# Attention and two feed-forward layers on one core: the second layer's row products held back, token parts spread over two pairs, later narrowing of weights

## The chip, the core and the metric

The kernel runs on one core of a Trainium2 chip. The engines are TensorE (matmuls, PE, and its weight loads, PEld), VectorE (DVE), ScalarE (ACT), GpSimd (POOL) and SyncE (SP), which issues most DMAs. The metric is the device time of one execution in microseconds (us). Everything is computed in float32; the weights of the two feed-forward layers arrive as float64.

## The reference

```
x = landmark_attention(q, k, v)          # 4 batches, 8 heads, 576 tokens, 64 per head -> 2304 x 512
x = (sigmoid(x @ w_gate) * (x @ w_val)) @ w_out          # 512 -> 1536 -> 512
h = x @ w_in                                             # 512 -> 2048
out = (max(h, 0) + alpha * min(h, 0)) @ w_out2           # 2048 -> 512
```

The attention has 32 landmarks per head, three softmaxes and six Newton steps for a pseudo-inverse. The output is 2304 x 512.

## The kernel before

**Split operands.** A float32 operand of a large matmul is held as a high part (the value rounded to the fast matmul format, a copy on ScalarE, line 124) and a low part (value minus high part, line 125, on VectorE, or on GpSimd where `lo="pool"`). Each product is then three matmuls: low times high, high times low, high times high (`TERMS`).

**First stage (to about 496 us).** Attention of batch 0, then 96 steps. A step is one block of 128 hidden features for half a batch (288 tokens): 12 matmuls of the gate and value products (`gv`, line 647), sigmoid and product, split, and, two steps later, 12 matmuls of the first layer's output (`acc`, line 666). Beside the steps run the attentions of the later batches, folding of attention matrices into weights (`psf`), and the preparation of the second stage. Its output goes to DRAM (`x2d`).

**Narrowing.** The second feed-forward layer's weights are 32 blocks of float64. `narrow_w2` loads one (`raw2`, two buffers), turns it into float32 with one or two ScalarE and two or three VectorE instructions (lines 139 to 151, the last writes `n2`, one buffer), and stores it to DRAM (`w2d`). In the program's text they begin at step `NARROW_FROM` with one every `NARROW_EVERY` steps. The two buffers lie in `apool` up to step 54; at step 55 that pool is given back and they lie in `rpool`. `rpool` is given back at step 83, and the pool `q2pool` (four homes for token parts, `xo2`) takes its room.

**Second stage.** Three groups `i` of 768 tokens, eight pairs `g` each; a pair is two blocks of 128 hidden features. The first product `x @ w_in` of a pair, a 2 x 2 block product (two feature blocks, two token halves of 384, two halves of the contraction), is made with seven block products instead of eight (`ORDER7` = 1, 2, 6, 7, 5, 4, 3). Each (`product`, line 950) is six matmuls of 384 columns into one of two PSUM banks (`gv`); VectorE adds (`plus`, line 1008) and one ScalarE copy (line 1015) read it out and free the bank. Four results h11, h22, h21, h12 come out per pair; `activated` takes each through two ScalarE instructions (lines 962, 963), one VectorE instruction (964) and a split into `g2s` or `g2r`. Each result then gives three parts of the second layer (`behind2`), a part being three matmuls of 512 columns (line 991) into one of six banks that accumulate over all 16 feature blocks; `catch_up2(n)` emits up to n parts. After a group's last pair the six banks are copied out (`store`, line 933).

**Token parts.** A group's tokens are loaded as four blocks (`load_x`, at pair 6 of the group before, line 770). Four VectorE subtractions of 128 x 768 (line 783) make the sums that seven products need, and seven operands of two halves each are split: 14 parts (`make_x7`, lines 124 and 125), which rotate through 15 homes. For groups 1 and 2 all this is written after pair 7, and the low half of every second part is on GpSimd. Parts, weights and tokens are named `x`, `w` and `xf` in the trace.

**Order.** Each engine works off its instructions in one fixed order. That order isn't the text's: the framework lays the work out ahead of time by text position and by when it takes operands and buffers to be ready. So an instruction can stand far from its place in the text.

Of the kernel before, what the change touches and what calls it, by code (L numbers as in the profile page):

```python
# [21 lines left out]
def tile_landmark_attention_glu_prelu(  # L22
# [46 lines left out]
    X2_LOAD, X2_SPLIT = 6, 7  # L69

    NARROW_FROM, NARROW_EVERY = 36, 1.4
# [611 lines left out]
    ORDER7 = (1, 2, 6, 7, 5, 4, 3)  # L683
    PLACE7 = {1: (0, 0), 2: (0, 1), 6: (1, 0), 5: (1, 1), 7: (2, 0), 3: (2, 1), 4: (3, 0)}
# [66 lines left out]
    def load_x(i):  # L751

        def room(first):
            if i == 0:
                if first:
                    t = home([P, 2, HG], F32, "xf")
                    return t
                return ws_tile("xf", (P, 2, HG), F32)
            if first:
                return wpool.tile([P, 2, HG], F32, tag="raw", name="xf", bufs=4)  # L760
            return ws_tile("xf", (P, 2, HG), F32)

        bs = {}
        for j, th in ((0, 0), (0, 1), (1, 1), (1, 0)):
            t = room(j == 0)
# [10 lines left out]
        bs["T2"] = room(False)  # L776
        xf[i] = bs

    def make_x7(i, ops):
        b11, b12, b21, b22, t2 = (xf[i][n] for n in ((0, 0), (0, 1), (1, 0), (1, 1), "T2"))  # L780

        def sub(out, x, y):
            nc.vector.tensor_tensor(out=out, in0=x, in1=y, op=ALU.subtract)

        for op in ops:
            if op == 6:

                sub(b11, b12, b11)
                sub(t2, b22, b11)
                sub(b12, b22, b12)  # L790
            if op == 4:

                sub(b21, b21, t2)
            src = {1: b11, 2: b21, 6: t2, 5: b11, 7: b12, 4: b21, 3: b22}[op]
            for kk in range(2):
                t = home([P, 2, HG], F32R, "x7")
                x7[i, op, kk] = t
                split(t, src[:, kk], lo="pool" if i > 0 and kk else "dve")
# [61 lines left out]
    for b in range(B):  # L860
# [5 lines left out]
        for i, (half, f, f0, f1) in enumerate(order):  # L866
# [45 lines left out]
            if at == X2_AT[0]:  # L912
                load_x(0)
                make_x7(0, ORDER7[:4])
            if at == X2_AT[1]:
# [5 lines left out]
                make_x7(0, ORDER7[4:])  # L921
# [20 lines left out]
    def product(i, g, op):  # L942
# [5 lines left out]
        for a, e in TERMS:  # L948
            for kk in range(2):
# [4 lines left out]
                n += 1  # L954
        return ps[:, :HG]
# [3 lines left out]
    def activated(h, f):  # L959
# [8 lines left out]
        if turn2[0] % 3:  # L968
# [6 lines left out]
    accs2, count, behind2 = {}, {}, deque()  # L975

# [3 lines left out]
    def catch_up2(n):  # L980

        for _ in range(min(n, len(behind2))):
# [56 lines left out]
    for i in range(NG):  # L1039
        for g in range(NF2 // 2):  # L1040
# [7 lines left out]
            if i + 1 < NG and g == X2_LOAD:  # L1048
                load_x(i + 1)
            pair(i, g)  # L1050
            if i + 1 < NG and g == X2_SPLIT:
# [33 lines left out]
```

## Time and profile before

| | us |
|---|---|
| median of three runs | 913.55 |
| lowest, highest | 912.08, 916.63 |
| the profiled execution | 911.39 |
| its span, first to last instruction | 909.6 |
| of it: up to the first matmul of line 950 | 495.9 |
| of it: second stage's matmuls | 407.7 |

The page of the profile gives busy time by engine, the table of stretches gives the same for any piece of the span (start and end, length, then busy time and number of instructions of PE, PEld, DVE, ACT and POOL, the granted TensorE clock as a share of full speed, the DMA engines' busy share, GB/s), the list of waits says which engine stood idle until what, and the timeline shows instructions in order. A busy TensorE isn't a TensorE at its peak, since matmuls are pipelined and their ends are modelled. So the spacing of matmul starts in a long run is read beside it.

### The profile page before, as it was taken

The numbers are of one execution on the slowest core, as the hardware profiler recorded it, in microseconds if no ns is written. First come the engines' busy times: TensorE is split into PE (matmuls) and PEld (weight loads), VectorE is DVE, ScalarE is ACT, GpSimd is POOL, SyncE is SP. The second block draws the span as 40 slices with busy tenths as digits, with TensorE's granted clock in tenths as the row PEclk, the third lists the DMA queues.
The fourth block names the chain that finished last, engine by engine and source line by source line (L and its number), as shares of the span: only waits on it lengthen the run. The fifth ranks groups of instructions, "written<-read, shape, count | busy, mean of one in ns | idle before, by whom it ended". The sixth has DMA issues, their size and how long they took to land.

```text
span 909.6 us, 15881 instructions
## 1 busy us (share of the span) xinstructions
PE 852.3 (94%) x6017; PEld 711.6 (78%) x6017; DVE 585.6 (64%) x1214; ACT 456.4 (50%) x981; POOL 83.7 (9%) x84
## 2 busy tenths in 40 slices
PE   5689889899999999998999999998999998999996
PEld 4367667677887877898999888886888877888884
DVE  3789988587665343779755787757554557554544
ACT  6676864465554333656544555644443435443433
POOL 0221112111011000230000000002000003000000
PEclk9679989999999999999999999999999999999999
DMA  9676878978431242888446446436432435552002
GB/s 270 218 234 185 252 248 240 285 222 255 132 95 54 94 143 90 264 253 256 161 166 236 150 172 210 144 111 204 128 132 93 127 106 197 173 173 93 1 1 69
DMA packets 98603, 150.98 MB, mean 166 GB/s; under 512 B 37328, under 2 KB 58336, under 8 KB 98528
## 3 DMA queue, kind: packets, MB, share of 16 engines
q1 hardware_dynamic: 95072, 137.40, 47.4%
q0 software_dynamic: 3456, 12.58, 4.4%
q8 instruction: 47, 0.77, 0.3%
q14 instruction: 28, 0.23, 0.1%
HBM read 108.01 MB, written 41.94 MB: 165 GB/s over the span
## 4 chain that ended last, share of the span: by engine, by line
PE 76%; DVE 9%; ACT 5%; DMA 5%; issue 3%; POOL 1%; SPq 1%; DVEq 0%; ACTq 0%; POOLq 0%
PE o L991 20%; PE acc L666 15%; PE gv L647 15%; PE prod L950 15%; PE psf L609 3%; PE psq L200 2%; DMA raw<-in_moe_w_in_dram 2%; DVE h L964 1%; PE psc L219 1%; PE psz L412 1%; PE psa L219 1%; DVE raw L148 1%; DVE h L1008 1%; PE psv L323 1%; DMA tk<-in_k_dram 1%
## 5 line engine op out<-in xcount | busy, mean ns | idle before, releaser
L950 PE MATMUL prod<-x,w 128*128 128x384 f32 x1008 | 195.9, 340 | 7.7 <-DVE u L1008 6.7
L647 PE MATMUL gv<-A,we 128*128 128x288 f32 x1152 | 194.9, 309 | 5.9 <-ACT g L658 3.4
L950 PEld LDWEIGHTS prod<-x,w 128*128 128x128 f32 x1008 | 176.8, 188 | 22.0 <-DVE u L1008 16.2
L647 PEld LDWEIGHTS gv<-A,we 128*128 128x128 f32 x1152 | 164.2, 193 | 36.3 <-issue 24.5
L666 PE MATMUL acc<-gs,wconv 128*128 128x288 f32 x1152 | 183.1, 302 | 6.6 <-DVE gs L125 3.1
L666 PEld LDWEIGHTS acc<-gs,wconv 128*128 128x128 f32 x1152 | 162.5, 191 | 19.1 <-issue 6.8
L991 PE MATMUL o<-w,g2s 128*128 128x512 f32 x576 | 148.3, 401 | 2.0 <-ACT g2s L124 1.2
L991 PEld LDWEIGHTS o<-w,g2s 128*128 128x128 f32 x576 | 105.2, 189 | 33.2 <-ACT g2s L124 7.2
L962 ACT ACTIVATE n<-h 128x384 f32<-128x384 f32 x96 | 50.4, 525 | 138.5 <-DVE h L1008 138.5
L991 PE MATMUL o<-w,g2r 128*128 128x512 f32 x288 | 74.6, 398 | 2.5 <-ACT g2r L124 1.9
L964 DVE SCALAR_TENSOR_TENSOR h<-n,minus_alpha,h 128x384 f32<-128x384 f32 x96 | 61.7, 643 | 16.2 <-ACT h L963 12.8
L658 ACT ACTIVATE g<-gv 128x288 f32<-128x288 f32 x96 | 39.3, 409 | 60.3 <-PE gv L647 57.2
L659 DVE TENSOR_TENSOR g<-g,gv 128x288 f32<-128x288 f32 x96 | 43.2, 450 | 38.6 <-PE gv L647 37.4
L124 ACT CAST gs<-g 128x288 fp32r<-128x288 f32 x96 | 41.5, 432 | 49.5 <-DVE g L659 48.8
L991 PEld LDWEIGHTS o<-w,g2r 128*128 128x128 f32 x288 | 52.2, 188 | 18.1 <-ACT g2r L124 5.3
L125 DVE TENSOR_TENSOR gs<-g,gs 128x288 fp32r<-128x288 f32 x96 | 50.2, 523 | 21.6 <-ACT gs L124 21.4
L1008 DVE TENSOR_TENSOR h<-u,prod 128x384 f32<-128x384 f32 x72 | 39.8, 552 | 34.9 <-PE prod L950 32.3
L139 ACT ACTIVATE raw<-raw 128x512 f32<-128x512 f32 x68 | 46.2, 680 | 30.6 <-DMA raw<-in_moe_w_in_dram 16.9
L1008 DVE TENSOR_TENSOR h<-p,prod 128x384 f32<-128x384 f32 x24 | 13.3, 554 | 66.4 <-PE prod L950 64.6
L148 DVE SCALAR_TENSOR_TENSOR raw<-raw 128x512 uint32<-128x512 uint32 x68 | 49.2, 734 | 9.1 <-ACT raw L143 8.3
L963 ACT ACTIVATE h<-h 128x384 f32<-128x384 f32 x96 | 50.4, 525 | 2.6
L125 POOL TENSOR_TENSOR x<-xf,x 128x384 fp32r<-128x384 f32 x14 | 15.9, 1141 | 335.7 <-ACT x L124 218.3
(137 smaller groups left out, 926.8 us busy)
## 6 DMA issues: line engine op xcount, KB each, us to landing
w<-w7d SPq DMA_DIRECT2D x48, 512.0 KB, 4.1
raw<-in_moe_w_out_dram SPq DMA_DIRECT2D x28, 512.0 KB, 4.9
wgv<-wgvd POOLq DMA_DIRECT2D x24, 512.0 KB, 5.0
w7d<-w SPq DMA_DIRECT2D x24, 512.0 KB, 2.7
raw<-in_moe_w_in_dram SPq DMA_DIRECT2D x16, 512.0 KB, 4.7
w2d<-n SPq DMA_DIRECT2D x32, 256.0 KB, 2.7
raw<-in_moe_w_gate_dram SPq DMA_DIRECT2D x24, 256.0 KB, 4.3
raw<-in_moe_w_val_dram SPq DMA_DIRECT2D x24, 256.0 KB, 4.7
```

The costliest lines, as they stand in the source:

```text
L125: (nc.gpsimd if lo == "pool" else nc.vector).tensor_tensor(out=dst[:, 1, :], in0=src, in1=f32(dst[:, 0, :]), op=ALU.subtract)
L139: nc.scalar.activation(w[:, :, 1], w[:, :, 1], AF.Copy, scale=2.0 ** -112)
L148: nc.vector.scalar_tensor_tensor(out=lo, in0=hi, scalar=0x80000000, in1=lo, op0=ALU.bitwise_and, op1=ALU.bitwise_or)
L647: nc.tensor.matmul(ps[:, :HB], lhsT=We[b, c, j][:, a, 256 * i + P * s : 256 * i + P * s + P], rhs=att[b, j, "A"][half][:, e, :], start=(n ...
L659: nc.vector.tensor_tensor(out=g, in0=g, in1=pss[1][:, :HB], op=ALU.mult)
L666: nc.tensor.matmul(acc[m][:, :HB], lhsT=wout_sb[f][:, a, P * m : P * m + P], rhs=gs[:, e, :], start=(f == f0 and n == 0), stop=(f == f1 - ...
L950: nc.tensor.matmul(ps[:, :HG], lhsT=w[:, a, kk], rhs=x7[i, op, kk][:, e], start=(n == 0), stop=(n == 5),)
L962: nc.scalar.activation(n, h, AF.Relu, scale=-1.0)
L963: nc.scalar.activation(h, h, AF.Relu)
L964: nc.vector.scalar_tensor_tensor(out=h, in0=n, scalar=minus_alpha[:, f : f + 1], in1=h, op0=ALU.mult, op1=ALU.add)
L991: nc.tensor.matmul(acc, lhsT=gs[:, a, P * t : P * t + P], rhs=w2_out[f][:, e, :], start=(count[i, u] == 1 and k == 0), stop=(count[i, u] = ...
L1008: nc.vector.tensor_tensor(out=c, in0=x, in1=ps, op=ALU.add)
```

## The change

1. `catch_up2` leaves at least six parts (`BEHIND`) of the second layer in the list; only the last call empties it.
2. The 14 token parts of the next group are written in the text between the products of two pairs: `X7_LAST` gives 3, 2, 2, 2, 1 after the first five products of pair 7, `X7_FIRST` 2, 2 after the first two of the next group's pair 0. All low halves are on VectorE. Three of the four subtractions (`sums_x`) are written after pair 6. One sum gets a buffer of its own (`T1`, of the tag `raw`) instead of overwriting a token block.
3. Every fifth instead of every third activated result goes to the tag `raw`.
4. Narrowing starts at step 50 with one every 0.95 steps, instead of step 36 with one every 1.4.

The number and shape of matmuls stay as they are.

```diff
--- before.py
+++ after.py
@@ -66,9 +66,13 @@
 
     X2_AT, W2_AT = (74, 83), (88, 91)
 
-    X2_LOAD, X2_SPLIT = 6, 7
-
-    NARROW_FROM, NARROW_EVERY = 36, 1.4
+    X2_LOAD = 6
+
+    BEHIND = 6
+
+    X7_LAST, X7_FIRST = (3, 2, 2, 2, 1, 0, 0), (2, 2, 0, 0, 0, 0, 0)
+
+    NARROW_FROM, NARROW_EVERY = 50, 0.95
 
     cpool = ctx.enter_context(tc.tile_pool(name="cpool", bufs=1))
     wpool = ctx.enter_context(tc.tile_pool(name="wpool", bufs=1))
@@ -681,6 +685,7 @@
 
     w7, w2_out = {}, {}
     ORDER7 = (1, 2, 6, 7, 5, 4, 3)
+    PARTS7 = [(op, kk) for op in ORDER7 for kk in range(2)]
     PLACE7 = {1: (0, 0), 2: (0, 1), 6: (1, 0), 5: (1, 1), 7: (2, 0), 3: (2, 1), 4: (3, 0)}
 
     def split2(dst, src, lo="dve"):
@@ -750,19 +755,16 @@
 
     def load_x(i):
 
-        def room(first):
-            if i == 0:
-                if first:
-                    t = home([P, 2, HG], F32, "xf")
-                    return t
-                return ws_tile("xf", (P, 2, HG), F32)
-            if first:
+        def room(n):
+            if n < 2 and i == 0:
+                return home([P, 2, HG], F32, "xf")
+            if n < 2 or n == 5:
                 return wpool.tile([P, 2, HG], F32, tag="raw", name="xf", bufs=4)
             return ws_tile("xf", (P, 2, HG), F32)
 
         bs = {}
-        for j, th in ((0, 0), (0, 1), (1, 1), (1, 0)):
-            t = room(j == 0)
+        for n, (j, th) in enumerate(((0, 0), (0, 1), (1, 1), (1, 0))):
+            t = room(n)
             at0, done = (2 * i + th) * HG, 0
             while done < HG:
                 bl, o = divmod(at0 + done, HB)
@@ -773,29 +775,34 @@
                 )
                 done += step
             bs[j, th] = t
-        bs["T2"] = room(False)
+        bs["T2"] = room(4)
+
+        bs["T1"] = room(5) if i > 0 else bs[0, 0]
         xf[i] = bs
 
-    def make_x7(i, ops):
-        b11, b12, b21, b22, t2 = (xf[i][n] for n in ((0, 0), (0, 1), (1, 0), (1, 1), "T2"))
-
-        def sub(out, x, y):
-            nc.vector.tensor_tensor(out=out, in0=x, in1=y, op=ALU.subtract)
-
-        for op in ops:
-            if op == 6:
-
-                sub(b11, b12, b11)
-                sub(t2, b22, b11)
-                sub(b12, b22, b12)
-            if op == 4:
-
-                sub(b21, b21, t2)
-            src = {1: b11, 2: b21, 6: t2, 5: b11, 7: b12, 4: b21, 3: b22}[op]
-            for kk in range(2):
-                t = home([P, 2, HG], F32R, "x7")
-                x7[i, op, kk] = t
-                split(t, src[:, kk], lo="pool" if i > 0 and kk else "dve")
+    def sub(out, x, y):
+        nc.vector.tensor_tensor(out=out, in0=x, in1=y, op=ALU.subtract)
+
+    def sums_x(i):
+        b11, b12, b22, t1, t2 = (xf[i][n] for n in ((0, 0), (0, 1), (1, 1), "T1", "T2"))
+        sub(t1, b12, b11)
+        sub(t2, b22, t1)
+
+        sub(b12, b22, b12)
+
+    def make_x7(i, op, kk):
+        if i == 0 and (op, kk) == (6, 0):
+            sums_x(i)
+        b11, b12, b21, b22, t1, t2 = (
+            xf[i][n] for n in ((0, 0), (0, 1), (1, 0), (1, 1), "T1", "T2")
+        )
+        if (op, kk) == (4, 0):
+
+            sub(b21, b21, t2)
+        src = {1: b11, 2: b21, 6: t2, 5: t1, 7: b12, 4: b21, 3: b22}[op]
+        t = home([P, 2, HG], F32R, "x7")
+        x7[i, op, kk] = t
+        split(t, src[:, kk])
 
     def home(shape, dtype, name):
         tag = homes.popleft()
@@ -911,14 +918,16 @@
                     narrow_pace -= 1
             if at == X2_AT[0]:
                 load_x(0)
-                make_x7(0, ORDER7[:4])
+                for op, kk in PARTS7[:8]:
+                    make_x7(0, op, kk)
             if at == X2_AT[1]:
                 assert not to_narrow
                 rpool.release()
                 q2pool = ctx.enter_context(
                     tc.tile_pool(name="q2pool", bufs=1, reuse_waits="tile")
                 )
-                make_x7(0, ORDER7[4:])
+                for op, kk in PARTS7[8:]:
+                    make_x7(0, op, kk)
             if at == W2_AT[0]:
                 make_w7(0)
             if at == W2_AT[1]:
@@ -952,6 +961,8 @@
                     start=(n == 0), stop=(n == 5),
                 )
                 n += 1
+        for _ in range(x7_pace.popleft() if x7_pace else 0):
+            make_x7(*x7_todo.popleft())
         return ps[:, :HG]
 
     turn2 = [0]
@@ -965,7 +976,7 @@
             out=h, in0=n, scalar=minus_alpha[:, f : f + 1], in1=h, op0=ALU.mult, op1=ALU.add
         )
         turn2[0] += 1
-        if turn2[0] % 3:
+        if turn2[0] % 5:
             gs = bpool.tile([P, 2, HG], F32R, tag="A", name="g2s", bufs=4)
         else:
             gs = wpool.tile([P, 2, HG], F32R, tag="raw", name="g2r", bufs=4)
@@ -973,13 +984,14 @@
         return gs
 
     accs2, count, behind2 = {}, {}, deque()
+    x7_todo, x7_pace = deque(), deque()
 
     def ready(i, f, th, gs):
         behind2.extend((i, f, th, t, gs) for t in range(3))
 
-    def catch_up2(n):
-
-        for _ in range(min(n, len(behind2))):
+    def catch_up2(n, done=False):
+
+        for _ in range(min(n, len(behind2) - (0 if done else BEHIND))):
             i, f, th, t, gs = behind2.popleft()
             u = 3 * th + t
             if (i, u) not in accs2:
@@ -1047,11 +1059,13 @@
                 load_w7(0)
             if i + 1 < NG and g == X2_LOAD:
                 load_x(i + 1)
+            if i + 1 < NG and g + 1 == NF2 // 2:
+                x7_todo.extend((i + 1, op, kk) for op, kk in PARTS7)
+                x7_pace.extend(X7_LAST + X7_FIRST)
             pair(i, g)
-            if i + 1 < NG and g == X2_SPLIT:
-                make_x7(i + 1, ORDER7)
-    while behind2:
-        catch_up2(1)
+            if i + 1 < NG and g == X2_LOAD:
+                sums_x(i + 1)
+    catch_up2(len(behind2), True)
 
 
 # ---- launch: one core; inputs and outputs as the reference has them ----
```

## Rows read from the trace of the kernel before

**Rows 1.** Page, part 1: busy time, share and instructions.

```profile
PE 852.3 (94%) x6017; PEld 711.6 (78%) x6017; DVE 585.6 (64%) x1214; ACT 456.4 (50%) x981; POOL 83.7 (9%) x84
```

**Rows 2.** Table of stretches; columns as explained in the section on the profile.

```profile
191.80:261.60 69.80, 68.36 (x787) 53.85 (x777) 52.87 (x144) 42.76 (x97) 10.51 (x11) 1.00 0.57 167
...
361.00:447.00 86.00, 81.55 (x602) 79.91 (x602) 66.79 (x115) 47.14 (x102) 16.47 (x12) 1.00 0.79 252
...
447.00:483.00 36.00, 36.00 (x275) 36.00 (x274) 21.41 (x49) 17.35 (x41) 0.00 (x0) 1.00 0.47 168
...
495.90:903.60 407.70, 395.47 (x1874) 333.97 (x1872) 245.34 (x443) 185.81 (x382) 15.90 (x14) 1.00 0.39 128
```

**Rows 3.** Stretches of second-stage pairs, the same columns.

```profile
522.30:603.90 81.60, 81.08 (x392) 69.58 (x391) 59.38 (x117) 43.90 (x90) 0.00 (x0) 1.00 0.50 172
...
603.90:624.10 20.20, 18.11 (x80) 15.02 (x79) 16.13 (x26) 10.87 (x26) 6.19 (x6) 0.92 0.29 99
...
624.10:643.10 19.00, 17.09 (x80) 13.73 (x79) 12.27 (x21) 9.82 (x21) 1.74 (x2) 1.00 0.78 245
...
643.10:724.80 81.70, 81.38 (x391) 69.56 (x391) 40.19 (x74) 31.16 (x64) 0.00 (x0) 1.00 0.32 104
...
724.80:779.90 55.10, 50.87 (x237) 41.23 (x236) 37.06 (x62) 27.53 (x59) 7.97 (x7) 1.00 0.53 172
...
779.90:878.00 98.10, 97.68 (x469) 83.40 (x468) 48.38 (x89) 37.53 (x77) 0.00 (x0) 1.00 0.25 84
...
878.00:903.60 25.60, 23.25 (x106) 18.58 (x105) 13.00 (x24) 10.82 (x22) 0.00 (x0) 1.00 0.11 30
```

**Rows 4.** TensorE's timeline, an ordinary pair: start, us, what.

```profile
679.05 4.25 PE L991 MATMUL o<-w,g2s 128*128 128x512 f32 x18
...
683.14 4.18 PE L950 MATMUL prod<-x,w 128*128 128x384 f32 x23
```

**Rows 5.** Waits, five ordinary pairs (643.1 to 724.8 us).

```profile
PEld prod L950 <- DVE u L1008: 1.8, 5, 0.4
...
PEld o L991 <- ACT g2s L124: 1.4, 4, 0.4
...
PEld o L991 <- DVE g2s L125: 1.0, 3, 0.3
```

**Rows 6.** Page, part 5: busy, mean ns of one | idle before.

```profile
L964 DVE SCALAR_TENSOR_TENSOR h<-n,minus_alpha,h 128x384 f32<-128x384 f32 x96 | 61.7, 643 | 16.2 <-ACT h L963 12.8
...
L1008 DVE TENSOR_TENSOR h<-u,prod 128x384 f32<-128x384 f32 x72 | 39.8, 552 | 34.9 <-PE prod L950 32.3
```

**Rows 7.** Timeline at the first change: VectorE stretched, TensorE waiting.

```profile
616.50 1.35 DVE L964 SCALAR_TENSOR_TENSOR h<-n,minus_alpha,h 128x384 f32<-128x384 f32 x1
...
618.37 1.01 PE L950 MATMUL prod<-x,w 128*128 128x384 f32 x2 [1.62 <-DVE u L1008]
```

**Rows 8.** Instructions that write x and xf: min/median/max ns.

```profile
L124 ACT CAST x<-xf x42: 493/510/535, 376.5 to 761.5; 128x384 fp32r<-128x384 f32 x42
...
L125 DVE TENSOR_TENSOR x<-xf,x x28: 544/552/1428, 377.9 to 760.8; 128x384 fp32r<-128x384 f32 x28
...
L783 DVE TENSOR_TENSOR xf<-xf x12: 946/948/2045, 395.5 to 753.3; 128x768 f32<-128x768 f32 x12
```

**Rows 9.** Narrowing groups (361 to 447 us): busy, mean | idle before.

```profile
L151 DVE SCALAR_TENSOR_TENSOR n<-raw 128x512 uint32<-128x512 uint32 x19 | 16.7, 879 | 1.8 <-DMA w2d<-n 1.7
...
L148 DVE SCALAR_TENSOR_TENSOR raw<-raw 128x512 uint32<-128x512 uint32 x19 | 13.1, 692 | 7.3 <-ACT raw L143 6.7
```

**Rows 10.** VectorE's timeline: the first and last of those 19.

```profile
368.77 0.69 DVE L151 SCALAR_TENSOR_TENSOR n<-raw 128x512 uint32<-128x512 uint32 x1
...
445.92 0.69 DVE L151 SCALAR_TENSOR_TENSOR n<-raw 128x512 uint32<-128x512 uint32 x1 [0.17 <-DMA w2d<-n]
```

**Rows 11.** Waits, 165 to 190 us: total, times, longest.

```profile
DVE n L151 <- DMA w2d<-n: 6.5, 2, 4.6
...
PE psq L200 <- DVE we L125: 3.6, 1, 3.6
```

## Prediction

> **What bounds the kernel now.** First the page: TensorE is busy 94% of the span, VectorE 64%, GpSimd 9% [rows 1]. So a gain must come from TensorE's waits, and I ask what the second stage would take without any. I read its timeline in an ordinary pair [rows 4]. A run of 18 second-layer matmuls lasts 4.25 us, the last one about 0.40 of it, so starts are (4.25 - 0.40)/17 = 0.2265 us apart. A run of 23 product matmuls lasts 4.18 us, the last one 0.34: (4.18 - 0.34)/22 = 0.1745 us. The stage has 3 x 8 x 7 x 6 = 1008 product matmuls and 96 x 3 x 3 = 864 of the second layer: 175.9 + 195.7 = 371.6 us. It takes 407.7 [rows 2]. So 36.1 us are waits, although TensorE counts as busy for 395.47 of the 407.70.
>
> Where they lie is read pair by pair [rows 3]. An ordinary pair has 42 and 36 matmuls: 7.33 + 8.15 = 15.48 us.
> - 16 ordinary pairs (5 + 5 + 6): 4.2 + 4.3 + 5.2 = 13.7 us over that, 0.86 each.
> - Five pairs at the two changes of group: 20.2 + 19.0 + 55.1 - 5 x 15.48 = 16.9 us.
> - The last pair with the tail of the second layer (105 weight loads, so 42 and 63 matmuls, 21.6 us): 4.0 us.
> - The first two pairs, by difference: 1.5 us.
>
> In five ordinary pairs the waits of TensorE's weight loads are 1.8 us on VectorE's adds that free a product bank and 1.4 + 1.0 us on the halves of a freshly made result [rows 5]. That is 4.2 us, 0.84 a pair, nearly the whole excess. The two rows of the timeline show how: 18 or more matmuls of the second layer in a lump, then 23 of the products in a row [rows 4]. In the lump TensorE waits for results just being split; in the row of products it waits for adds.
>
> **Six parts behind.** No matmul is added. Six parts are 6 x 3 x 0.2265 = 4.08 us of TensorE work whose operands are finished. In the text's order a pair becomes: products 1, 2, one part, 6, one, 7, one, 5, two, 4, two, 3, five. A part (0.68 us) or two lies between the freeing of a bank and its next use, and an add takes 0.55 us [rows 6]. A result's parts come at least six parts after it is listed, while making it takes about 3.3 us: the add 0.55 and line 964 0.64 [rows 6], and three ScalarE instructions and a low half of 0.5 to 0.55 each, as those of the token parts [rows 8]. So both waits of rows 5 should go. I leave 0.15 us per pair, since timing on the chip is not that of the text: 16 x 0.15 = 2.5 us in place of 13.7. Bounds: 0, and half of today's waits, 6.9. In the tail the chain of the last result (3.3 us) now stands behind eight or more parts: 0.5 in place of 4.0 (0.3 to 2). The first two pairs have little to hold back: 1.5 stays (1 to 3).
>
> **Every fifth result in `raw`.** At a change three of the four `raw` buffers hold token blocks and the new sum. One result in five fits the fourth: a result lives for less than a pair (about 12 us from split to last use), and five results take 1.25 pairs. The other four buffers hold four of five. In the text's order at most four results are alive. Cost nothing; if a buffer were late, TensorE would still have the parts behind.
>
> **Token parts over two pairs.** Pairs around a change carry more VectorE work: 16.13 us in a pair of 20.2 [rows 3]. Some of it is stretched: line 964 took 1.35 us there [rows 7] against a mean of 0.64 [rows 6], and TensorE then waited 1.62 us for an add [rows 7]. After the change GpSimd has nothing to do here. VectorE in pair 7: an ordinary pair has 40.19/5 = 8.04 us [rows 3], plus ten low halves at 0.55 us [rows 8], 13.6 us of 15.5. In pair 0: 8.04, plus four low halves 2.2, one subtraction 0.95 [rows 8] and three copies of the output, which I put at 0.7 each as something over a low half, 13.3 us. The three subtractions (2.85 us) go to pair 6, which has room. ScalarE gets ten copies of 0.51 us [rows 8] in pair 7, on 31.16/5 = 6.23 us [rows 3]: 11.3 us, no bound. But there they stand in front of work that frees banks. Behind the two copies that wait for product 1's last matmul stands its bank's own copy: 3 x 0.51 = 1.5 us, against product 2 and one part, 1.05 + 0.68 = 1.73 us. That just fits. The low halves wait on VectorE for ScalarE and hold adds up in the same way. The price comes from two rows: ordinary pairs of group 0 carry 59.38/5 = 11.9 us of VectorE work at no extra wait, and the pair with 16.13 us lost 4.7 [rows 3]. By a line between them 13.6 us costs about 1.5 and 13.3 about 1.2. Both changes together: 5.0 us in place of 16.9 (1.5 to 12.5).
>
> The Trainium skill (SBUF — State Buffer, "Two separate sides" and "Who interferes with whom") calls the port pair that VectorE and GpSimd share an exclusive lock: the loser stands for the other's whole instruction when VectorE reads two SBUF operands. The 1.35 against 0.64 us agrees [rows 6, 7]. Against this change speaks TensorE: Matmul & The Clock Gate (its opening table), which lists VectorE's queue as strictly first in, first out: a low half that waits for its ScalarE copy then holds all adds behind it. If each of ten waited 0.5 us, pair 7 would need 13.6 + 5 = 18.6 us of VectorE and lose 3.1 us instead of 1.5, 3.2 us more over both changes. That stays inside my bounds.
>
> **Narrowing from step 50.** What counts is not the start but how many fall to each pool. Before: steps 36 to 54 at one per 1.4 steps give 13 in `apool`, and 19 in `rpool`; the trace has those 19 after 361 us [rows 9]. After: steps 50 to 54 give 5, and 27 in `rpool`. The 19 start their last instruction from 368.77 to 445.92 us [rows 10], 77.15/18 = 4.29 us apart, wider than a step (12 + 12 matmuls of 288 columns, about 3.2 us by the 275 in 36 us [rows 2]). The text's own pace is 1.4 x 3.2 = 4.5 us, so these rows don't tell whether text or buffers hold them. I take the buffers (two for loads, one for results), as the first narrowings stood for a store [rows 11]; then the new `EVERY` doesn't speed them up. If it was the text, 27 at 3.0 us end near 447 us, and eight more cost the same, earlier. The 27th then comes at 368.8 + 26 x 4.29 = 480 us, not 446. Into 447 to 483 us come eight more narrowings, at least 0.88 + 0.69 us of VectorE each [rows 9], 12.6 us on 21.41, of 36.00 [rows 2]. TensorE's idle time between 361 and 447 us was 86.00 - 81.55 = 4.45 us [rows 2], 0.23 per narrowing: eight more cost 1.9 us (0 to 6). Earlier, eight of the 13 go away, the last ones. TensorE idled 1.44 us from 191.8 to 261.6 us [rows 2]: I take half, a gain of 0.7 us. At most the gain is 5: between 165 and 190 us a narrowing stood 4.6 us on VectorE for its buffer's store, and TensorE lost 3.6 us behind it [rows 11]. That is the fourth or fifth, which the change keeps.
> The late end also moves the last token parts of group 0: their homes lie where the narrowing's buffers were. Product 5 needs one at 495.9 + 24 x 0.1745 = 500.1 us, its split takes about 1.3 us, so about 18 us are free. Cost nothing, and one microsecond for each late one after that.
>
> **The rivals.**
> - The margin is eaten: the framework lets TensorE take parts whenever a product isn't ready, so the list is often empty and ordinary waits stay. For: today's lumps aren't in the text either, which has one part after each of products 2, 6 and 7. Against: parts are needed only when products wait, and 4 us is more than any ordinary wait. It leaves 13.7 + 4.0 + 1.5, and at changes 5 x 0.86 + 5.0: a gain of 7.6 us, so about 907.
> - Narrowing late, middling: at 5.4 us each the 27th comes at 509 us and product 5 waits 10 us: 898. For: VectorE nearly full from 447 us. Against: 4.29 is measured where it was busy 66.79 of 86.00 us [rows 2].
> - Slower, by the same mechanism: from about 5.0 us apart (26 x 5.0 + 368.8 = 499) each further 0.1 us costs 2.6 us. Over 918 us it takes 30 us of wait, 6.15 us apart, 1.4 times the measured pace.
> - More than forecast: changes and pairs without waits and 4 us early, about 875. For: every wait of rows 5 has its cause removed. Against: VectorE at 88% around a change.
> - The parts bring nothing and narrowing costs what the rest brings: within 0.5%.
>
> **How the numbers follow.** Second stage: waits 36.1 become 2.5 + 5.0 + 0.5 + 1.5 = 9.5, a gain of 26.6 us (11.7 with all upper bounds: 6.9 + 12.5 + 2 + 3; 33.3 with all lower). First stage: 1.9 - 0.7 = 1.2 us lost. 911.4 - 26.6 + 1.2 = 886.0 for an execution like the profiled one. The median of three lies 2.2 above that one: 888. Chances: forecast (876 to 897) 0.64; margin eaten 0.10, half of it within 0.5%; narrowing middling 0.14; slower 0.05; more 0.05; nothing 0.02. The range 876 to 903 takes in the forecast and nearly all of the middling case. 0.5%, 4.6 us, is about what a measurement can tell from no change. Faster by more: 0.64 + 0.14 + 0.05 + 0.05 = 0.88; within: 0.07; slower: 0.05.
>
> **What would show it.** Right: ordinary pairs of 15.5 to 15.7 us; no weight load that waits for a split; parts mixed with products in the timeline, not in lumps of 18; pairs at a change under 17.5 us; 27 narrowings after 361 us with a last one near 480; step 1 of the second stage within 3 us of 496. Wrong: ordinary pairs still at 16.3 (margin eaten); a wait of product 5 for a token part near 500 us (narrowing); pair 7 above 18 us with VectorE full (low halves).

## The result, and the profile after

The changed kernel takes 886.77 us (median; 885.81 to 889.74) beside 913.57 for the kernel before on the same chip: ratio 0.9708, 95% interval 0.9674 to 0.9742. The forecast was 888.0, the range 876 to 903. Its profiled execution took 886.35 us with a span of 884.6, so 25.0 less than before. By stage: the second stage's matmuls gained 30.8 us (407.7 to 376.9), the stretch up to the first product lost 5.1 (495.9 to 501.0), and the stretch after the last matmul lost 0.7. The net hides a loss as large as a sixth of the gain.

The page, part 1 (against [rows 1]), shows TensorE at the same share of a shorter span, and less work on GpSimd:

```profile
PE 834.6 (94%) x6017; PEld 717.5 (81%) x6017; DVE 582.9 (66%) x1228; ACT 461.5 (52%) x981; POOL 68.4 (8%) x70
```

Stretches of the kernel after (columns as in [rows 2]). The first four stand against [rows 2] (the third runs to the first product), the others are pairs, against [rows 3]: the last pair of group 0, the first of group 1, four ordinary pairs, the last pair.

```profile
191.80:261.60 69.80, 67.38 (x775) 53.06 (x769) 44.57 (x127) 37.36 (x88) 9.57 (x11) 1.00 0.38 100
361.00:447.00 86.00, 80.96 (x585) 78.83 (x584) 64.51 (x115) 47.51 (x103) 17.51 (x12) 0.98 0.81 259
447.00:501.00 54.00, 52.51 (x394) 51.81 (x393) 38.02 (x83) 28.49 (x64) 0.00 (x0) 1.00 0.68 231
501.00:877.90 376.90, 376.84 (x1873) 338.71 (x1872) 246.50 (x462) 192.24 (x385) 0.00 (x0) 1.00 0.44 143
...
606.80:622.50 15.70, 15.70 (x79) 14.08 (x78) 14.00 (x29) 11.23 (x25) 0.00 (x0) 1.00 0.49 159
622.50:638.20 15.70, 15.70 (x79) 14.13 (x79) 9.61 (x18) 7.58 (x15) 0.00 (x0) 1.00 0.74 228
653.90:716.70 62.80, 62.80 (x313) 56.53 (x312) 32.84 (x61) 27.27 (x53) 0.00 (x0) 1.00 0.37 117
857.90:877.90 20.00, 19.94 (x97) 17.32 (x95) 9.88 (x18) 8.22 (x16) 0.00 (x0) 1.00 0.08 22
```

In the second stage TensorE stands idle for 0.06 of 376.90 us. Every pair from the second to the 23rd takes 15.66 to 15.73 us, those at the changes of group too (20.2 and 19.0 before). TensorE's timeline in an ordinary pair (start, us, what; against [rows 4]) shows parts and products mixed instead of two long lumps:

```profile
656.03 0.86 PE L1003 MATMUL o<-w,g2s 128*128 128x512 f32 x3
656.73 1.22 PE L959 MATMUL prod<-x,w 128*128 128x384 f32 x6
...
666.18 3.60 PE L1003 MATMUL o<-w,g2s 128*128 128x512 f32 x15
```

The waits around the first change of group (606.8 to 638.2 us: total, times, longest; against [rows 5], and against the 1.62 us wait of [rows 7]). VectorE and ScalarE wait; of TensorE the list has one wait of 0.2 us, of its weight loads:

```profile
DVE h L1020 <- PE prod L959: 1.8, 2, 0.9
DVE x L129 <- ACT x L128: 1.4, 1, 1.4
...
PEld prod L959 <- DVE u L1020: 0.2, 1, 0.2
```

The narrowing is the other side (361 to 501 us, groups with their idle time, against [rows 9]). There are now 27, and their last instruction starts 4.14 us apart, from 369.2 to 476.9 us:

```profile
L155 DVE SCALAR_TENSOR_TENSOR n<-raw 128x512 uint32<-128x512 uint32 x27 | 21.3, 789 | 3.0 <-DMA w2d<-n 2.8
...
L143 ACT ACTIVATE raw<-raw 128x512 f32<-128x512 f32 x27 | 18.4, 683 | 19.9 <-DMA raw<-in_moe_w_out_dram 10.4 <-DMA raw<-in_moe_w_in_dram 9.2
```

**Where the 5.1 us went.** Up to step 57 both kernels are level (362.4 before, 362.8 after). From there to the first product it takes 133.5 and 138.2 us; first the row of before, then that of after:

```profile
362.40:495.90 133.50, 129.05 (x962) 127.41 (x961) 95.55 (x180) 70.06 (x156) 16.47 (x12) 1.00 0.67 223
```

```profile
362.80:501.00 138.20, 131.68 (x963) 128.84 (x962) 101.70 (x196) 75.49 (x165) 17.51 (x12) 0.99 0.76 247
```

TensorE idles 6.52 us instead of 4.45, which makes 2.1 of the 4.7 us; and it is busy 2.6 us longer with the same matmuls. Most of that is the granted clock. Two stretches of after, around step 75, and the same two of before:

```profile
418.00:425.00 7.00, 4.84 (x36) 4.46 (x34) 7.00 (x15) 5.87 (x14) 0.00 (x0) 1.00 0.71 231
425.00:429.00 4.00, 3.41 (x14) 3.07 (x15) 4.00 (x10) 2.44 (x7) 0.00 (x0) 0.57 0.64 208
```

```profile
418.00:425.00 7.00, 5.51 (x40) 5.08 (x39) 7.00 (x16) 5.00 (x13) 0.00 (x0) 1.00 0.81 269
425.00:429.00 4.00, 4.00 (x31) 3.87 (x31) 4.00 (x10) 3.44 (x9) 0.00 (x0) 1.00 0.95 298
```

VectorE is full in both, as narrowing meets the loads and sums of group 0's tokens. TensorE idled 2.16 us of seven in after and 1.49 in before. Then in after it ran at the lower of its levels (1.2 GHz) for most of the second stretch, in before not at all. At 0.57, four microseconds lose 0.43 x 4 = 1.7 us.

The timeline of after has the wait just ahead of it. A half batch of steps ends there, and its accumulators are copied out (line 863) before their banks take the next one:

```profile
423.33 0.67 ACT L143 ACTIVATE raw<-raw 128x512 f32<-128x512 f32 x1
423.90 0.66 ACT L147 ACTIVATE raw<-raw 128x512 uint32<-128x512 uint16 x1
...
424.78 0.39 ACT L863 COPY xs<-acc 128x288 f32<-128x288 f32 x1
...
425.22 0.47 PEld L670 LDWEIGHTS acc<-gs,wconv 128*128 128x128 f32 x3 [2.61 <-ACT xs L863]
425.22 0.82 PE L670 MATMUL acc<-gs,wconv 128*128 128x288 f32 x3 [2.38 <-DVE x L129]
```

TensorE's weight load waits 2.61 us for ScalarE's copy of the first bank. The profile puts the matmul's own wait down to VectorE, which was at the low half of a token part; but that ended within 0.01 us of the copy (425.18 and 425.17 us), and the matmul reads no token part. In front of the copy ScalarE works off two instructions of a narrowing, 1.33 us together. In before the copy stands at 423.64 us, ahead of the next narrowing, and TensorE's wait for it is 1.49 us.

### The profile page after: what moved, and what is told of

The parts are those of the page before. It is cut to its first block, busy times and chain, and to the rows that moved or that the text cites. A ratio compares the mean times of both kernels' runs of the same rounds, so it can differ in the third digit from the quotient of the medians.

```text
span 884.6 us, 15890 instructions
## 1 busy us (share of the span) xinstructions
PE 834.6 (94%) x6017; PEld 717.5 (81%) x6017; DVE 582.9 (66%) x1228; ACT 461.5 (52%) x981; POOL 68.4 (8%) x70
## 4 chain that ended last, share of the span: by engine, by line
PE 75%; DMA 11%; DVE 7%; ACT 3%; issue 2%; SPq 1%; POOL 1%; DVEq 0%; ACTq 0%
PE o L1003 22%; PE prod L959 20%; PE gv L651 12%; PE acc L670 11%; PE psf L613 3%; DMA raw<-in_moe_w_in_dram 3%; DMA raw<-in_moe_w_gate_dram 2%; DMA raw<-in_moe_w_out_dram 2%; DVE raw L152 1%; DMA w2d<-n 1%; PE psq L204 1%; PE psz L416 1%; ACT raw L143 1%; PE psv L327 1%; DVE n L155 1%
## 5 line engine op out<-in xcount | busy, mean ns | idle before, releaser
L959 PE MATMUL prod<-x,w 128*128 128x384 f32 x1008 | 199.8, 337 | 0.0
L959 PEld LDWEIGHTS prod<-x,w 128*128 128x128 f32 x1008 | 180.4, 188 | 12.7 <-DVE u L1020 0.2
L1003 PE MATMUL o<-w,g2s 128*128 128x512 f32 x693 | 180.5, 393 | 0.0
L1003 PEld LDWEIGHTS o<-w,g2s 128*128 128x128 f32 x693 | 128.3, 188 | 19.9 <-ACT g2s L128 0.2
L975 DVE SCALAR_TENSOR_TENSOR h<-n,minus_alpha,h 128x384 f32<-128x384 f32 x96 | 59.1, 617 | 55.3 <-ACT h L974 54.8
L128 ACT CAST g2s<-h 128x384 fp32r<-128x384 f32 x77 | 39.4, 513 | 49.7 <-DVE h L975 49.7
L129 DVE TENSOR_TENSOR g2s<-h,g2s 128x384 fp32r<-128x384 f32 x77 | 42.7, 556 | 13.2 <-ACT g2s L128 11.2
L1003 PE MATMUL o<-w,g2r 128*128 128x512 f32 x171 | 45.2, 393 | 0.0
L613 PE MATMUL psf<-wgv,m 64*32 64x512 f32 x384 | 42.3, 620 | 0.6 <-DVE wgv L155 0.3
```

The lines of the kernel that those rows point to most:

```text
L128: nc.scalar.copy(dst[:, 0, :], src)
L129: (nc.gpsimd if lo == "pool" else nc.vector).tensor_tensor(out=dst[:, 1, :], in0=src, in1=f32(dst[:, 0, :]), op=ALU.subtract)
L613: nc.tensor.matmul(pss[j][LM * h : LM * h + LM], lhsT=att[b, j, "M"][d, u], rhs=wgv[c, j][d, u], start=True, stop=True,)
L959: nc.tensor.matmul(ps[:, :HG], lhsT=w[:, a, kk], rhs=x7[i, op, kk][:, e], start=(n == 0), stop=(n == 5),)
L975: nc.vector.scalar_tensor_tensor(out=h, in0=n, scalar=minus_alpha[:, f : f + 1], in1=h, op0=ALU.mult, op1=ALU.add)
L1003: nc.tensor.matmul(acc, lhsT=gs[:, a, P * t : P * t + P], rhs=w2_out[f][:, e, :], start=(count[i, u] == 1 and k == 0), stop=(count[i, u] = ...
```

## Experiments

The second stage is the stretch from the first to the last matmul of lines 950 and 991 (959 and 1003 in after); e1 to e12 are experiments 1 to 12; "from step 57" is the time from that step to the first product, 133.5 us before and 138.2 after. "The margin" is the six parts held back, "the changes" are the two changes of group.

**1. The change with the narrowing as before** (`e1_narrow_as_before`).

```diff
-    NARROW_FROM, NARROW_EVERY = 50, 0.95
+    NARROW_FROM, NARROW_EVERY = 36, 1.4
```

> The changed kernel with one part undone: narrowing begins at step 36 with one every 1.4 steps again. Theory: the later narrowing costs the first stage 5.1 us (first product at 501.0 against 495.9 us) and gives the second stage nothing. Then the first product is back at 495.5 to 496.5 us, the second stage stays 376 to 378 us, and the time is about 881.5 us, 5 under the changed kernel. Rival: the second stage needs the later narrowing, or the 5 us come from another part of the change; then the time stays at 885 to 888 us.

886.74 us, ratio 0.9692 (0.9651 to 0.9732). Second stage 377.2, from step 57 135.8. The trace gives 2.4 us back, the median none: the first 360 us alone differ by some microseconds between executions (step 57 begins between 359.7 and 367.5 us in the eight profiles that have the narrowing as before). So this first comparison left it open.

**2. Only the late narrowing** (`e2_narrow_only`, against the kernel before).

```diff
-    NARROW_FROM, NARROW_EVERY = 36, 1.4
+    NARROW_FROM, NARROW_EVERY = 50, 0.95
```

> The kernel before with the later narrowing alone (from step 50, every 0.95). Theory: 27 narrowings instead of 19 after 361 us, about 4.2 us apart, the last near 477 us; the first product moves from 495.9 to 500 to 502 us, the second stage keeps 407 to 408 us, so about 918.5 us (plus 5). Rival: narrowing is neutral by itself, 913 to 914.5 us.

920.31 us, ratio 1.0071 (1.004 to 1.0102): slower by itself. From step 57 138.9 us, second stage 406.7, about as before (407.7). Its profile loses another 3.8 us up to step 57 (366.2 against 362.4), which lies within that spread. The part that lost is found, and it acts ahead of the second stage alone.

**3. Only the parts behind** (`e3_behind_only`, against the kernel before).

```diff
-    def catch_up2(n):
+    def catch_up2(n, done=False):
...
-        for _ in range(min(n, len(behind2))):
+        for _ in range(min(n, len(behind2) - (0 if done else 6))):
...
-    while behind2:
-        catch_up2(1)
+    catch_up2(len(behind2), True)
```

> The kernel before with six parts of the second layer held back, nothing else. Theory: ordinary pairs fall from 16.3 to 15.7 us (16 of them, 10 us) and the last pair loses its 3 to 4 us; the pairs at a change still have the lump of splits on GpSimd and VectorE, and keep 4 to 10 of their 12 us over ordinary pairs. Time 890 to 898 us. Rival 1, the margin is eaten: ordinary pairs stay at 16.2 or more, 907 to 911 us. Rival 2, the six parts cover the changes too, and the spreading is not needed: all pairs 15.7 to 15.8 us, 881 to 883 us.

887.87 us, ratio 0.97 (0.9658 to 0.9741): less than the theory's 890 to 898, more than the 881 to 883 of the second rival. The rows are the last pair of group 0 and the first of group 1, with GpSimd still at work:

```profile
600.40:617.00 16.60, 16.19 (x80) 13.99 (x79) 14.09 (x23) 10.77 (x24) 7.71 (x6) 1.00 0.36 115
617.00:633.30 16.30, 15.96 (x80) 14.06 (x79) 11.56 (x21) 8.13 (x17) 1.13 (x1) 1.00 0.82 256
```

Ordinary pairs take 15.69. The second stage takes 380.2, so 27.5 of the 30.8 us come from the margin alone. The changes gain by it too: their pairs take 16.57 and 16.31 us, where the kernel before took 20.2 and 19.0. I had expected less of it there.

**4. Only the spreading** (`e4_spread_only`: experiment 1 without the margin).

```diff
-    BEHIND = 6
+    BEHIND = 0
```

> The changed kernel with no part held back (BEHIND 0) and the narrowing of before: the spread token parts on VectorE alone, the buffer for a sum and every fifth result in raw remain. Theory: ordinary pairs stay at 16.2 to 16.4 us and the last pair keeps its 4 us; the five pairs at changes lose 3 to 8 of their 12 us over ordinary pairs: 905 to 911 us. Rival: without the six parts VectorE's fuller pairs cost what the spreading saves, 912 to 916 us.

907.98 us, ratio 0.9945 (0.9917 to 0.9973). Ordinary pairs are back at 16.34, the pairs at the changes at 16.1 to 19.2, the last at 25.55; second stage 400.7. Against before that is 7.0 us from the spreading (with VectorE alone at the low halves). On top of the margin it is 3.0 (380.2 to 377.2). Both parts remove some of the same waits.

**5 to 7. The same three kernels side by side** on one chip: the change (`e5_change_again`, no edit), experiment 1 (`e6_narrow_as_before_again`), experiment 3 (`e7_behind_only_again`).

> The changed kernel itself once more, beside the next three on one chip, to tell 3 to 5 us apart. Both theories: ratio to the kernel before 0.969 to 0.973.

> The changed kernel with the narrowing of before, timed again beside it. The pieces of the traces after step 57 give the late narrowing a cost of about 3 us in the first stage, while the first 360 us wander by several us from execution to execution. Theory: the cost is real, 2 to 5 us under the changed kernel on the same chip, ratio about 0.966. Rival: nothing that can be told apart, within 1.5 us of it.

> Six parts held back alone, timed again. Theory: the spreading of token parts is worth the 1.4 us per change of group that its trace shows beside the changed kernel's (16.57 and 16.31 us against 15.74 and 15.69), so this is about 3 us over the changed kernel with the narrowing of before. Rival: spreading costs as much in the first stage (the subtractions' and buffers' new order at step 74) as it brings at the changes; then the two are within 1.5 us.

888.64 (ratio 0.9731, 0.9704 to 0.9758), 885.26 (0.9695, 0.9669 to 0.9721) and 885.45 (0.9708, 0.968 to 0.9736). The early narrowing lies 3.4 us under the change, with intervals that just overlap. The traces agree on the place: from step 57 140.3, 133.8 and 135.7 us. The 3 us of the spreading stand in the second stage (377.2 against 380.2), but the medians lie 0.2 us apart: in the time it wasn't told from nothing.

**8. Narrowing much earlier** (`e8_narrow_early`), so that only one falls behind step 57.

```diff
-    NARROW_FROM, NARROW_EVERY = 50, 0.95
+    NARROW_FROM, NARROW_EVERY = 24, 1.0
```

> The changed kernel with narrowing moved the other way: from step 24 with one every step, so 31 of 32 are written before the pool is given back at step 55. Theory: TensorE's waits after step 57 come from narrowings in the queues of ScalarE and VectorE; with one left there, the excess of the steps from 57 to 94 over 3.18 us (6 to 11 us in the runs so far) falls to 1 to 4 us, and the narrowings run between 155 and 350 us, where VectorE is 45% busy from 262 us on; the time falls 3 to 6 us under the changed kernel with the narrowing of before, to 878 to 882 us. Rival: the same waits come up earlier, among the attention's short chains, and the time is the same or up to 5 us more.

899.95 us, ratio 0.9864 (0.9832 to 0.9895): missed by 20 us in total, and half right. A stretch that lies wholly behind step 57, then the waits that matter from 310 to 360 us:

```profile
370.00:510.00 140.00, 140.00 (x1071) 136.15 (x1070) 72.89 (x145) 60.29 (x139) 16.73 (x12) 1.00 0.35 116
```

```profile
PEld gv L651 <- DVE we L129: 6.9, 2, 4.9
PE gv L651 <- DVE we L129: 6.4, 2, 4.7
DVE n L155 <- DMA w2d<-n: 5.6, 5, 2.0
```

From step 57 it takes 127.1 us without one wait of TensorE: with narrowing gone from there, all of them are gone. Steps 36 to 56 take 122.5 instead of 100.4. The timeline shows one of the waits:

```profile
358.10 0.69 DVE L155 SCALAR_TENSOR_TENSOR n<-raw 128x512 uint32<-128x512 uint32 x1 [2.04 <-DMA w2d<-n]
358.70 1.28 DVE L129 TENSOR_TENSOR we<-psf,we 128x512 fp32r<-128x512 f32 x2
...
359.44 1.85 PE L651 MATMUL gv<-A,we 128*128 128x288 f32 x12 [1.73 <-DVE we L129]
```

VectorE stands 2.04 us until the store has read the single result buffer; the folded weights' split stands in its queue behind that; TensorE waits 1.73 us for the split. The longest wait, 4.69 us up to 345.90 us, begins otherwise: ScalarE's narrowing waits 2.98 us for a load, VectorE's 3.04 us for ScalarE's, and again the split stands behind. So what makes TensorE wait here is a narrowing that waits in an ordered queue, for its store or for its load. Experiment 12 takes away a wait for the store, but behind step 57.

The waits aren't all of the 22 us: 8.9 are idle time of TensorE, and 8.5 go to a lower clock. Of these, 5.1 lie between 289 and 300 us, where TensorE didn't stand at all (10.30 us busy of 10.30, granted clock 0.50). Experiment 4, with narrowing as before, lost 5.1 us at the same place; so that part isn't shown to be narrowing's.

**9. A margin of three parts** (`e9_margin_3`, narrowing as in experiment 1).

```diff
-    BEHIND = 6
+    BEHIND = 3
```

> Three parts held back instead of six, narrowing of before, all else as changed. Theory 1, a result only has to be listed its making time (about 3.3 us) before its first use: with three parts and the three products written between, 5 us lie between, so ordinary pairs stay at 15.69 us and the second stage at 377 to 378 us. Theory 2, the finished work itself must be longer than the making time: three parts are 2.1 us, so ordinary pairs are 15.9 to 16.2 us, the second stage 382 to 388 us.

893.34 us, a single time; second stage 388.0. Ordinary pairs take 15.79 to 15.84, so three parts do for them. The changes don't hold; the last pair of group 0, the first of group 1, an ordinary one:

```profile
605.80:617.30 11.50, 11.50 (x61) 10.48 (x60) 9.75 (x20) 8.14 (x19) 0.00 (x0) 1.00 0.43 139
617.30:639.80 22.50, 18.54 (x90) 15.62 (x89) 13.41 (x26) 10.62 (x22) 0.00 (x0) 1.00 0.75 234
...
657.70:673.50 15.80, 15.80 (x80) 14.01 (x79) 8.23 (x16) 6.74 (x13) 0.00 (x0) 1.00 0.37 116
```

The short pair has 18 second-layer matmuls instead of 36, the next 45 and 4 us of waits (605 to 658 us):

```profile
ACT n L973 <- DMA out_dram<-ob: 8.9, 2, 4.6
...
PE o L1003 <- ACT g2s L128: 4.0, 2, 2.7
```

ScalarE stands until a store of the finished group's output has read its buffer, since those copies share buffers with fresh results; so the results come late. Neither theory held alone: ordinary pairs hold with three parts, the change of group needs more.

**10. Every second low half on GpSimd again** (`e10_gpsimd_halves`, narrowing late).

```diff
-        split(t, src[:, kk])
+        split(t, src[:, kk], lo="pool" if i > 0 and kk else "dve")
```

> The changed kernel with the low half of every second token part of groups 1 and 2 on GpSimd again. Theory: with the parts spread, both engines have room and the six parts cover the stretched VectorE instructions; pairs at a change 15.7 to 15.9 us. Rival: GpSimd's halves are what the two changes cost when only the parts are held back (16.57 and 16.31 us): pairs at a change 16.2 to 16.6 us.

892.29 us, a single time, so the trace decides. The last pairs of groups 0 and 1 take 17.06 and 17.16 us instead of 15.7, all others as after; second stage 379.7, so 2.8 us more. That is over the rival's 16.2 to 16.6 us too. The timeline at the first change:

```profile
615.08 1.02 POOL L129 TENSOR_TENSOR x<-xf,x 128x384 fp32r<-128x384 f32 x1 [1.19 <-ACT x L128]
615.10 1.41 DVE L975 SCALAR_TENSOR_TENSOR h<-n,minus_alpha,h 128x384 f32<-128x384 f32 x1
...
617.50 0.79 PE L959 MATMUL prod<-x,w 128*128 128x384 f32 x3 [1.10 <-DVE u L1020]
```

Line 975 takes 1.41 us beside GpSimd's instruction, against a mean of 0.617 on the page of after, and TensorE then waits 1.10 us for an add. As told for [rows 7], the Trainium skill (SBUF — State Buffer, "Who interferes with whom") has VectorE stand for GpSimd's whole instruction: here line 975 began 0.02 us after GpSimd's instruction and ended 0.41 us behind its end (616.51 and 616.10 us), which agrees. What it lost by this is 0.79 us beside an instruction of 1.02.

**11. VectorE alone, without the spreading** (`e11_lump_on_vector`: experiment 3 with one more edit).

```diff
-                split(t, src[:, kk], lo="pool" if i > 0 and kk else "dve")
+                split(t, src[:, kk])
```

> Six parts held back, token parts in one lump after pair 7 as before, but every low half on VectorE. Theory: the 1.4 us that a change of group costs with the lump are GpSimd's doing; without it the pairs are 15.7 to 15.9 us. Rival: they come from the lump, seven more low halves and four subtractions queued at once on VectorE, then 16.3 to 17.5 us.

886.21 us, a single time; second stage 379.2. Group 0's last pair, then the first two pairs of group 1 and of group 2:

```profile
604.40:620.10 15.70, 15.70 (x79) 14.13 (x78) 14.25 (x28) 9.82 (x22) 0.00 (x0) 1.00 0.35 117
620.10:652.20 32.10, 31.59 (x157) 28.15 (x156) 21.05 (x39) 16.85 (x34) 0.00 (x0) 1.00 0.67 214
746.40:779.00 32.60, 31.64 (x158) 28.19 (x157) 21.10 (x39) 16.82 (x34) 0.00 (x0) 1.00 0.73 233
```

Two ordinary pairs take 31.4 us, so 0.7 and 1.2 us are left, where experiment 3 lost 1.5 at each change. So the theory holds in part: GpSimd's halves are 0.8 and 0.3 of those 1.5 us, the lump is the rest. TensorE's longest wait in the second pair of group 1 is 0.8 us, of a weight load for the copy of an output bank (line 933). Of the 3.0 us by which the spreading and VectorE improve on the margin, 1.0 comes from taking GpSimd off and then 2.0 from the spreading. In the other order GpSimd's share is 2.8 (experiment 10).

**12. Two result buffers for narrowing** (`e12_two_result_buffers`: experiment 1 with a second `n2` in `rpool`; one home of token parts moves to the later pool for the room).

```diff
-        t = pool.tile([P, NW], F32, tag="n2", name="n2", bufs=1)
+        t = pool.tile([P, NW], F32, tag="n2", name="n2", bufs=2 if rpool else 1)
...
-    homes = deque(["xo"] * 11 + ["xo2"] * 4)
+    homes = deque(["xo"] * 10 + ["xo2"] * 5)
...
-        return pool.tile(shape, dtype, tag=tag, name=name, bufs=11 if tag == "xo" else 4)
+        return pool.tile(shape, dtype, tag=tag, name=name, bufs=10 if tag == "xo" else 5)
```

> The changed kernel with the narrowing of before and, after step 55, two buffers for the narrowed block instead of one (a home for token parts moves from the first pool to the second to make room). Theory: the waits after step 57 are instructions queued behind a narrowing that waits for its store; the stretch from step 57 to the first product falls from 133.8 to 135.8 us to 130 to 133 us, the time 2 to 4 us under the kernel with one buffer (ratio about 0.966). Rival: they come from waits for loads on ScalarE, and nothing changes, ratio 0.968 to 0.972.

882.41 us, ratio 0.9649 (0.9613 to 0.9685): faster than the kernel before, and than the change as measured in experiment 5 (0.9704 to 0.9758; the first comparison's 0.9674 to 0.9742 just touches). Both comparisons take in the earlier narrowing. The same narrowing with one buffer has 0.9692 (0.9651 to 0.9732) and 0.9695 (0.9669 to 0.9721) in experiments 1 and 6, and these intervals overlap the new one; so by the time alone the second buffer isn't told from nothing. The trace goes further: from step 57 it takes 131.2 us, less than all eight profiles with the same narrowing and one buffer (133.5 to 136.7).

```profile
L155 DVE SCALAR_TENSOR_TENSOR n<-raw 128x512 uint32<-128x512 uint32 x19 | 16.7, 877 | 0.1
```

VectorE's wait for the store is gone (1.8 us in [rows 9]), and TensorE idles 131.2 - 128.5 = 2.7 us instead of 4.45, with as much work on VectorE. ScalarE's waits for the loads remain (7.5 and 5.9 us in its groups of line 143). The moved home wasn't tried by itself.

**All traces together.** From step 57 on, the profiles differ in two things: TensorE's idle time, and how often its clock fell to the lower of its levels. The loss by falls is the sum of (1 - granted clock) over stretches of one microsecond.

| narrowing | idle us | lost by falls, us | length us |
|---|---|---|---|
| as before: before, e1, e3, e4 | 4.4, 4.7, 4.1, 4.5 | 0, 1.7, 1.7, 3.4 | 133.5, 135.8, 134.6, 136.7 |
| as before: e6, e7, e9, e11 | 4.6, 5.2, 4.4, 4.6 | 0, 1.7, 0, 0 | 133.8, 135.7, 133.5, 133.8 |
| late: after, e2, e5, e10 | 6.5, 5.9, 6.4, 6.1 | 1.7, 3.4, 5.1, 1.7 | 138.2, 138.9, 140.3, 136.9 |
| two buffers: e12 | 2.7 | 0 | 131.2 |
| early: e8 | 0.0 | 0 | 127.1 |

Both losses taken off the length leave 128.5 to 130.0 us in every profile but e8's (127.1), so they account for most of what differs. Late narrowing adds 6.2 - 4.6 = 1.6 us of idle time and 3.0 - 1.1 = 1.9 us of lower clock, of 3.9 in all. Falls come with early narrowing too, only more seldom: so one profile of each kernel would give this loss as anything from 0.2 (e10 against e4) to 6.8 us (e5 against before). With four profiles against eight, the 1.9 is a mean of few falls.

Of the 1.6 us of idle time, 0.9 lie at one place. At the change of half batch some 62 us behind step 57, the four profiles with late narrowing all have two instructions of a narrowing on ScalarE in front of the copy that frees the first bank, and TensorE waits 2.2 to 2.4 us; in the eight with narrowing as before none is in front, and it waits 1.0 to 1.5. The clock falls near such waits: 10 of the 11 stretches at the lower level begin within 3 us of a wait for a bank, at this change or at the one some 19 us behind step 57.

## Why the prediction came out right

**The second stage, measured against its steps** (us over the floor, the 371.6 us that the prediction has for the stage without waits):

| step | before | predicted | measured |
|---|---|---|---|
| 16 ordinary pairs | 13.7 | 2.5 | 3.4 |
| five pairs at the changes | 16.9 | 5.0 | 1.1 |
| last pair | 4.0 | 0.5 | 0.4 |
| first two pairs | 1.5 | 1.5 | 0.5 |
| sum | 36.1 | 9.5 | 5.3 |

- **Six parts behind.** Right: e3 shows the whole mechanism by itself, and e4 its absence. The 0.21 us left per pair aren't waits, as the prediction had it. They are the spacing of the starts. In the pair from 653.93 to 669.62 us the 36 second-layer matmuls take 8.31 us, each counted to the next start, and the 42 of the products 7.38: 0.231 and 0.1757 us apiece, against 0.2265 and 0.1745 in the long lumps of [rows 4]. That makes 0.16 + 0.05 = 0.21 us. My floor was taken from runs that the change abolishes, and nearly all of the 5.3 us is this.
- **The rival that the margin is eaten** (907) fell: with six parts TensorE's weight loads wait 0.4 us for results in the whole second stage, and with three the waits that count lie at the changes (e9).
- **The changes of group** are the term that was mis-sized: 5.0 against 1.1. The step that failed is the line of prices over VectorE's load. Its upper point, the pair with 16.13 us of VectorE work, lost 4.7 us by three things: a clock of 0.92 (0.08 x 20.2 = 1.6 us, in [rows 3], which I didn't use; the same pair of e2, without a fall of the clock, took 18.98), GpSimd's stretching of VectorE (e10 puts its share at 1.4 per change), and waits without a margin. None of them is a price of VectorE's load: 14.00 of 15.70 us cost nothing. The arithmetic was off as well. By the two points as written, 11.9 at nothing and 16.13 at 4.7, the line gives 1.9 and 1.6 us, 6.9 for both changes; the 1.5 and 1.2 need the 0.86 of an ordinary pair taken off first, and twice their sum is 5.4, not 5.0. The schedule also put 13 low halves in pair 7, not ten.
- **Which part does it** was wrong too. The forecast put the 11.9 us of gain at the changes down to the spreading and to VectorE alone. The margin alone takes those five pairs from 16.9 to 4.0 us over the floor (e3), and both together add 3.0 to that in the second stage.
- **VectorE's queue in order.** The Trainium skill (TensorE: Matmul & The Clock Gate, the opening table) lists VectorE's queue as strictly first in, first out; by that I had weighed low halves that wait in front of adds, with 18.6 us for pair 7. The only such wait listed at the first change is 1.4 us, and the pair took 15.7. That doesn't speak against the order of the queue, which e8 shows at work; but here its instructions were seldom late, and six parts lay between.
- **Every fifth result in `raw`** cost nothing, as said: no wait for a buffer appears among those of TensorE.
- **Narrowing's pace.** Right: 27 after 361 us, 4.14 us apart where 4.29 was assumed, the last at 476.9 where 480 was. The text's pace is now 3.0, so the text doesn't set it. Product 5 didn't wait, and the two rivals built on its wait fell.
- **Narrowing's price** failed: 1.2 us forecast, 5.1 measured. The idle time was sized rightly (1.9; 2.1 in the profile of after, 1.6 over all traces), though not as 0.23 us for each narrowing: more than half of it is one wait, where a narrowing came in front of ScalarE's copy of a bank. 5.1 lies inside the bound of 6. Missing was what can follow a wait: the lower clock, 1.7 us in the profile of after. The relief of 0.7 us earlier didn't come (0.4 lost up to step 57). About 0.9 us of longer busy time stays unexplained.

So the margin's mechanism was right, but that the time came within 1.2 us was luck, since errors cancelled: the forecast had 4.2 us too little gain in the second stage, 3.9 too little loss in the first, and nothing for the stretch after the last matmul, which lost 0.7. They bring 886.0 to about the profile's 886.35; of the 2.2 added for the median 0.4 were needed. What stays open: why some of these waits are followed by a fall and others, as long, aren't (before waited 1.49 us at the second change of half batch without one, e1 1.42 us with one; e10 idled 2.6 us from 383 to 390 us without one). That wasn't tried. And the medians don't resolve the spreading's 3 us.

## What to carry to other kernels

Hold back a few instructions with finished operands on the bounding engine, and size that stock by the worst stretch (here the change of group), not by the ordinary one. Work moved out of sight still occupies ordered queues: two instructions on ScalarE in front of the copy of a bank made TensorE wait 0.9 us longer, and a single buffer in front of a store made VectorE, and behind it TensorE, wait. So look at what will stand ahead of the instruction that frees a bank, and give such side work a second buffer where there is room. Allow for the clock that may follow a wait of TensorE.

## What was unexpected in the hardware

- After waits of TensorE the granted clock fell, down to 0.50 in stretches of one microsecond, and a fall cost 1.7 us beside the wait itself, one of them 3.4; e5 lost 5.1 us in this way between 384 and 433 us. In e8 it fell from 289 to 300 us too, where no wait came first: from 283.7 to 289 us TensorE's timeline has mostly small matmuls (lines 312, 327 and 416), without a gap.
- One GpSimd subtraction of 1.02 us stretched a VectorE instruction from 0.62 to 1.41 us. An add that reads one operand from PSUM wasn't stretched: at 612.94 us of e10 line 1020 took 0.54 us, wholly beside a GpSimd subtraction. Token parts' low halves on VectorE took 818 ns (mean of six, 609.9 to 642.7 us) beside GpSimd, and 553 ns without:

```profile
L129 DVE TENSOR_TENSOR x<-xf,x 128x384 fp32r<-128x384 f32 x6 | 4.9, 818 | 1.9 <-ACT x L128 1.9
```

```profile
L129 DVE TENSOR_TENSOR x<-xf,x 128x384 fp32r<-128x384 f32 x13 | 6.8, 553 | 1.4 <-ACT x L128 1.4
```
